# Hash-masked attention ahead of two expert layers: two of twelve score tiles transposed by TensorE in their own banks, a bias by a scalar operand, output scaling on GpSimd, and a new order of stages

## The chip, the cores and the metric

The program runs on one core of a Trainium2 chip. The metric is the device time of one execution in microseconds (us); three executions of the kernel before stand behind its median. A measurement of this kernel can tell about 0.3% (4.6 us) from no change.

## What is computed

Attention comes first, for 2 batches of 8 heads with 768 positions and 64 values per head. A position only attends to positions whose 6-bit hash bucket is the same:

```
q_bucket = bits of (q @ proj > 0);  k_bucket = bits of (k @ proj > 0)
mask     = q_bucket[:, None] == k_bucket[None, :]
scores   = where(mask, q @ k.T / 8, -1e9)
attn     = exp(scores - max(scores)); attn /= sum(attn) + 1e-9
out      = attn @ v
```

The result (1536 tokens of 512 values) goes through an expert layer that sums all eight experts, each token weighted by a matrix that is normalized eight times along rows and columns, and then through a second expert layer that gives each token that passes a threshold to one expert and adds its output. All results are float32.

## The kernel before, in words

`attention` handles 8 pairs of heads, one after the other. A pair has 12 **units**: (pair, head, block of 128 query rows), so 96 units in all. What happens to a unit, with the lines of the kernel before:

- `scores` (L243): four float32r matmuls of 384 columns write 128 x 768 scores into a two-bank PSUM tile, one of three (`p`, `s0`, `s1`). The hash mask is part of the product, so that a masked entry is off by 2^33 times the number of differing bits.
- `max_` (L252 to L254): VectorE reduces the row minimum, makes a scale (0 or -1) and a bias from it. Both small results are one value per partition.
- `exp_` (L261): ScalarE writes the float32 exponentials `P` to SBUF and gives the score tile back. `P` has three buffers.
- `hi` (L266) and `lo` (L269): ScalarE casts `P` to float16, GpSimd subtracts that from `P`; both halves go to `Pq` (six buffers).
- `trans` (L273): one DMA transpose on SP's queue turns both halves into `T` (nine buffers), 12 blocks of 128 x 128.
- `av` (L284, L285): twelve matmuls of `T` with the values, which are split into three bfloat16 parts with a column of ones; two units share a PSUM bank.
- `fin` (L295 to L298): for two units at once, VectorE sums the three parts, takes the reciprocal of the row sum and multiplies, into `X`. `xt` (L306, L307) transposes a finished pair's `X` for the expert layers.

Beside it runs the preparation of the next pair (`prep`): transposes of k and q into a score tile (`T`, L174), high parts on ScalarE (`A`, L180), low parts on VectorE (`Dd`, L184), copies to other partitions by DMA (`dup`, L188), the hash products into a score tile (`zz`, L199), their signs (`sgn`, L211), four small DMAs of them on SP (`sd`, L207), and the split of v (`v0` to `v3`, L203 and L230 to L232). The preparation takes score tiles from the same three.

The order on every engine is the order in which the program writes the stages down; each engine works through its own queue in that order and waits where a result is missing. A loop over `n` writes, for each step, the stages of `STEP[n % 2]`, each for the unit `n - lag`, and the pieces of preparation that the table `PLAN` hangs behind a place of the period of twelve steps. `scores` is written while a score tile is free, at most two units ahead (`AHEAD`). A step's list before, and how `give` and `take` hand the score tiles on:

```
STEP = [[('av', 7), ('max', 0), ('fin', 8), ('trans', 4), ('exp', 0), ('lo', 2), ('hi', 0), ('scores', -1)], ...]
while nxt <= min(n + AHEAD, N - 1) and free and ("sd", units[nxt][0]) in done:
    scores(units[nxt])
```

In the last two thirds of attention the loop also starts pieces of the expert layers' setup (`next(m)`); their weights are loaded on SP as well. After attention the expert layers fill the rest of the time.

Of the kernel before, what the change touches and what calls it, by code (L numbers as in the profile page):

```python
# [13 lines left out]
ALU = mybir.AluOpType  # L14
# [3 lines left out]
BIG = float(2.0 ** 33)  # L18
# [14 lines left out]

STEP = [[('av', 7), ('max', 0), ('fin', 8), ('trans', 4), ('exp', 0), ('lo', 2), ('hi', 0), ('scores', -1)], [('av', 7), ('max', 0), ('lo', 2), ('fin', 8), ('trans', 4), ('exp', 0), ('scores', -1), ('hi', 0)]]

PLAN = {12: 'Tk Ak1', 14: 'Ak0', 21: 'dk1', 25: 'Dk0 Dk1 Tq', 33: 'dk0', 37: 'Aq0 v0', 45: 'Dq0 Aq1', 49: 'Dq1', 59: 'z0', 60: 'z1', 66: 'dq1', 72: 'dq0 sg', 83: 'sd', 92: 'x v1', 94: 'v2', 95: 'v3'}
FIRST = "Tk Tq Ak0a Ak1a Dk0a Dk1a Ak0b Ak1b dk0 dk1 Dk0b Dk1b Aq0a Aq1a Dq0a Dq1a Aq0b Aq1b dq0 dq1 Dq0b Dq1b load1 za zb sga sgb sd load"
V0 = {1: "v0", 2: "v1", 3: "v2", 4: "v3"}  # L40

# [2 lines left out]
AHEAD = 2  # L44
M0 = range(39, 75, 3)
LD0, LDM, NTB, WARM = 3, 1, 9, 18


def attention(nc, tc, ident, q, k, v, proj, xT, m, go):
    with ExitStack() as c:  # L50
# [5 lines left out]
        free = ["p", "s0", "s1"]  # L56
        held = {}

        def take(key):
            t = held[key] = free.pop(0)  # L60
            return (pB if t == "p" else pS).tile([128, 2, 512], F32, tag=t, name=t, bufs=1)

        def give(key):
            free.append(held.pop(key))
# [84 lines left out]
        vs = {}  # L149

        def prep(i):

# [47 lines left out]

            def v0():
                nc.gpsimd.memset(vt[:, :, :, 0:1], 1.0)
                nc.vector.tensor_copy(out=vt[:, :, :, 1:65], in_=inp[i][2])  # L203
# [16 lines left out]
            for x, a in (("a", 0), ("b", 1)):  # L220
# [66 lines left out]
        def fin(u):  # L287
# [43 lines left out]
        stage = {"max": max_, "exp": exp_, "hi": hi, "lo": lo, "scores": scores, "trans": trans, "av": av, "fin": fin}  # L331
# [22 lines left out]
        for n in range(-1, N + AVLAG + 2):  # L354
            i, off = divmod(n + 13, 12)
            if off == 0 and i < NP:
                cur = prep(i)
            for j, (st, lag) in enumerate(STEP[n % 2]):
                u = n - lag
                if st == "scores":  # L360
                    while nxt <= min(n + AHEAD, N - 1) and free and ("sd", units[nxt][0]) in done:
                        scores(units[nxt])
                        nxt += 1
                elif 0 <= u < N and not (n > N and st in ("lo", "trans")) and not (st == "fin" and u >= N - AVLAG):
                    assert st != "av" or ("v3", units[u][0]) in done
                    stage[st](units[u])
                for op in PLAN.get(8 * off + j, "").split():
# [5 lines left out]
                if j == 7 and n in V0:  # L373
                    todo.extend((op, 0, p0[op]) for op in V0[n].split())
                prepare()
            if n >= 0 and n % 12 == LD0 and n // 12 + 2 < NP:
                ld.append(load(n // 12 + 2))
            if n % LDM == 0 and ld and next(ld[0], 0) == 0:
                ld.pop(0)
            if n in M0:  # L380
                next(m)
            if n == N:
                for u in units[N - 8:]:
                    if u in PP:
                        lo(u)
                for u in units[N - 8:]:
                    if u in PT and u not in TT:
                        trans(u)
                cp.close()
                cl.close()  # L390
                free[:] = ["p"]
            if 0 <= n - N < AVLAG:
                fin(units[n - AVLAG])
            if n == N + AVLAG:
                xt(NP - 1)
            if n >= N:
                next(m)
# [895 lines left out]
```

## Time and profile before

| | |
|---|---|
| runs | median 1525.09 us of 3 (1522.27 to 1526.89) |
| the profiled execution | 1523.56 us, its span 1521.7 us |
| mean granted TensorE clock | 0.975 of full speed |
| busy share of the span | TensorE 93%, VectorE 59%, GpSimd 59%, ScalarE 43% |
| attention | from the start to about 300 us |

The page gives the busy share of each engine over the whole span; the shares are a mean over attention and two expert layers, which have different limits, so the stretch of attention is read by itself. A stretch is here a period of twelve units, cut at the start of the row minimum that follows the hash signs (L211), which come once in twelve units. In windows by stretch, "DMA share" is packet time over 16 engines and can pass 1 where packets overlap.

### The profile page before, as it was taken

Reading aid. Unit: us, or ns where it says so; the run is one execution under the profiler, and the core shown is the slowest. Engines: PE = TensorE matmul, PEld = TensorE weight load, DVE = VectorE, ACT = ScalarE, POOL = GpSimd, SP = SyncE. Lnnn points to the kernel's source line nnn. Section 1 sums busy time; section 2 is a strip of 40 time slices with the busy share of each in tenths; the row PEclk is TensorE's granted clock in tenths of the full one; section 3 lists DMA queues with packets and bytes.
Section 4 is the critical chain, followed back from the end, with each engine's and each line's share of the span. In section 5 each row is a group of like instructions: output and inputs, shape, how many; then the busy total and the mean of one; then the engine's idle time right before and its main releaser. Section 6 shows DMA issues by size and latency. Waiting matters only on the chain.

```text
span 1521.7 us, 21039 instructions
## 1 busy us (share of the span) xinstructions
PE 1415.9 (93%) x7747; PEld 1240.7 (82%) x7747; DVE 899.5 (59%) x1778; ACT 653.8 (43%) x1015; POOL 895.9 (59%) x763
## 2 busy tenths in 40 slices
PE   6788777799999999999999999999999999998997
PEld 5677666578889889899898888989899898876886
DVE  7899989977625336254264736426244262555876
ACT  4777767742423333233333433333133232325665
POOL 3666666764665767657677656856667565512111
PEclk7999999999999999999999999999999999999999
DMA  5999999902121121211211412121211212527762
GB/s 148 192 207 202 203 200 183 171 30 82 57 83 56 56 83 57 83 56 56 84 56 56 164 58 56 56 83 56 83 56 56 84 56 84 194 67 241 258 249 69
DMA packets 224224, 166.27 MB, mean 109 GB/s; under 512 B 160023, under 2 KB 199063, under 8 KB 219761
## 3 DMA queue, kind: packets, MB, share of 16 engines
q1 hardware_dynamic: 219520, 154.69, 38.2%
q10 hardware_dynamic: 2448, 5.58, 1.7%
q0 software_dynamic: 2144, 4.57, 0.9%
q8 instruction: 63, 1.03, 0.3%
q14 instruction: 49, 0.39, 0.1%
HBM read 113.04 MB, written 7.77 MB: 79 GB/s over the span
## 4 chain that ended last, share of the span: by engine, by line
PE 59%; DVE 19%; POOL 15%; issue 3%; ACT 2%; DMA 1%; ACTq 0%; POOLq 0%; DVEq 0%
PE mp L1158 30%; PE mp L1041 15%; POOL w L473 8%; DVE m L252 5%; PE mp L935 4%; PE mp L954 4%; DVE m L254 3%; PE mp L1132 2%; DVE X L298 2%; POOL w L488 2%; POOL T L465 1%; DVE r L296 1%; POOL T L464 1%; DVE t L184 1%; PE mp L912 1%
## 5 line engine op out<-in xcount | busy, mean ns | idle before, releaser
L1158 PE MATMUL mp<-w,h 128*128 128x512 f32 x2160 | 501.5, 393 | 0.0
L1041 PE MATMUL mp<-x,w 128*128 128x384 f32 x2688 | 479.9, 337 | 14.5 <-POOL w L473 9.3
L1041 PEld LDWEIGHTS mp<-x,w 128*128 128x128 f32 x2688 | 467.2, 188 | 22.9 <-POOL w L473 14.1
L1158 PEld LDWEIGHTS mp<-w,h 128*128 128x128 f32 x2160 | 404.5, 188 | 85.8
L488 POOL TENSOR_TENSOR w<-raw,w 128x512 fp32r<-128x512 f32 x127 | 177.4, 1397 | 235.3 <-ACT w L487 235.3
L487 ACT CAST w<-raw 128x512 fp32r<-128x512 f32 x256 | 151.2, 620 | 193.3 <-PE mp L1158 175.1
L1175 DVE SCALAR_TENSOR_TENSOR acc<-mp,Pm,acc 128x512 f32<-128x512 f32 x78 | 54.1, 749 | 291.9 <-PE mp L1158 291.9
L269 POOL TENSOR_TENSOR Pq<-P,Pq 128x768 f16<-128x768 f32 x96 | 158.2, 1653 | 94.7 <-ACT Pq L266 87.0
L473 POOL TENSOR_TENSOR w<-raw,w 128x512 fp32r<-128x512 f32 x124 | 128.9, 1060 | 95.5 <-ACT w L469 95.5
L1085 ACT ACTIVATE h<-ca 128x768 fp32r<-128x768 f32 x64 | 54.3, 848 | 235.4 <-DVE ca L1049 235.4
L473 POOL TENSOR_TENSOR w<-T,w 128x1024 fp32r<-128x1024 f32 x62 | 149.7, 2415 | 0.0
L471 ACT CAST w<-T 128x1024 fp32r<-128x1024 f32 x64 | 67.3, 1052 | 174.2 <-POOL T L466 170.4
L243 PE MATMUL s<-k,t 128*128 128x384 f32 x264 | 70.4, 393 | 37.0 <-ACT P L261 31.7
L284 PE MATMUL b<-vt,T 128*128 128x193 bf16 x576 | 98.8, 261 | 2.5 <-DMA T<-Pq 2.5
L1049 DVE TENSOR_TENSOR u<-mp,p 128x384 f32<-128x384 f32 x64 | 35.6, 556 | 103.2 <-ACT p L1056 61.0
L285 PE MATMUL b<-vt,T 128*128 128x129 bf16 x576 | 95.1, 229 | 0.0
L488 DVE TENSOR_TENSOR w<-raw,w 128x512 fp32r<-128x512 f32 x129 | 84.3, 696 | 12.7 <-ACT w L487 12.5
L261 ACT ACTIVATE P<-s,m 128x768 f32<-128x768 f32 x66 | 65.4, 991 | 55.0 <-DVE m L254 35.1
L243 PEld LDWEIGHTS s<-k,t 128*128 128x128 f32 x264 | 48.7, 211 | 46.4 <-ACT P L261 38.8
L266 ACT CAST Pq<-P 128x768 f16<-128x768 f32 x96 | 79.9, 832 | 6.2 <-DMA T<-Pq 3.8
L1089 DVE SCALAR_TENSOR_TENSOR h<-ca,h 128x768 fp32r<-128x768 f32 x64 | 66.5, 1039 | 19.3 <-ACT h L1085 19.3
L1049 DVE TENSOR_TENSOR u<-mp,u 128x384 f32<-128x384 f32 x128 | 66.7, 553 | 18.6 <-PE mp L1041 14.1
(268 smaller groups left out, 1924.5 us busy)
## 6 DMA issues: line engine op xcount, KB each, us to landing
raw<-in_moe_w_dram SPq DMA_DIRECT2D x128, 256.0 KB
raw<-in_moe_w_dram SPq DMA_DIRECT2D x64, 512.0 KB
raw<-in_moe_w_dram SPq DMA_DIRECT2D x32, 1024.0 KB
k<-in_k_dram SPq DMA_DIRECT2D x16, 192.0 KB
q<-in_q_dram SPq DMA_DIRECT2D x16, 192.0 KB
v<-in_v_dram SPq DMA_DIRECT2D x8, 384.0 KB
out_dram<-acc SPq DMA_DIRECT2D x2, 1536.0 KB
k<-k ACTq DMA_DIRECT2D x14, 192.0 KB
```

The lines of the kernel that those rows point to most:

```text
L243: nc.tensor.matmul(ps[:, hf, 0:384], lhsT=a[s][h][:, js], rhs=b[s][h][:, 384 * hf:384 * hf + 384], start=n == 0, stop=n == 1)
L252: nc.vector.tensor_reduce(out=m[:, 0, c], in_=w2(ps), axis=AX.XY, op=ALU.min)
L266: nc.scalar.copy(out=PT[u][:, 0], in_=PP[u])
L269: nc.gpsimd.tensor_tensor(out=PT[u][:, 1], in0=PP.pop(u), in1=PT[u][:, 0], op=ALU.subtract)
L284: nc.tensor.matmul(o, lhsT=t[:, n, :], rhs=vt[:, h, ORDER[n], :], start=n == 0, stop=False)
L285: nc.tensor.matmul(o[:, 0:129], lhsT=t[:, 6 + n, :], rhs=vt[:, h, ORDER[n], 0:129], start=False, stop=n == 5)
L473: tl(out=w[:, 1, c0:c1], in0=src, in1=wf[:, 0, c0:c1], op=ALU.subtract)
L487: nc.scalar.copy(out=w[:, 0, :], in_=v)
L488: eng.tensor_tensor(out=w[:, 1, :], in0=v, in1=w[:, 0, :].bitcast(F32), op=ALU.subtract)
L1041: nc.tensor.matmul(dst, lhsT=w[:, i_, 2 * blk + c, :], rhs=x[:, x_, c, :], start=n == 0, stop=n == 5)
L1049: nc.vector.tensor_tensor(out=o, in0=a, in1=b_, op=ALU.add)
L1158: nc.tensor.matmul(ys[t], lhsT=h[:, a, 128 * t:128 * t + 128], rhs=w[:, i_, :], start=i == 0 and n == 0, stop=i == 7 and n == 2)
```

## The change

- In each pair, the units 2 and 8 (`QP`; all but the last two units of the program may be among them) keep their score tile after `exp_`. TensorE transposes the float32 `P` back into that tile (`qtrans`, six transposes), ScalarE casts it from there to `T` (`qhi`), VectorE writes the low half to `T` (`qlo`), and only then the tile is given back. These units have no `hi`, no `lo` and no DMA transpose.
- The bias is made by a `tensor_scalar` with the row minimum as both input and scalar operand, in place of a `scalar_tensor_tensor`.
- The multiplication at the end of `fin` goes to GpSimd, except for the last seven units.
- The lists of stages and `PLAN` are new; `PLAN` now hangs on the stages' names. `lo` comes one step after its unit and not two, `trans` five steps and not four.

```diff
-STEP = [[('av', 7), ('max', 0), ('fin', 8), ('trans', 4), ('exp', 0), ('lo', 2), ('hi', 0), ('scores', -1)], ...
+STEP = [[('max', 0), ('exp', 0), ('trans', 5), ('ql', 2), ('fin', 8), ('hi', 0), ('qh', 1), ('av', 7), ('qt', 0), ('lo', 1), ('scores', -1)],
+        [('trans', 5), ('ql', 2), ('max', 0), ('exp', 0), ('scores', -1), ('fin', 8), ('qh', 1), ('hi', 0), ('lo', 1), ('av', 7), ('qt', 0)]]
-PLAN = {12: 'Tk Ak1', 14: 'Ak0', ...
+PLAN = {(0, 'max'): 'Tk', (0, 'lo'): 'Ak1', (1, 'ql'): 'Ak0', ...
+QP = (2, 8)
-            nc.vector.scalar_tensor_tensor(out=m[:, 2, c], in0=m[:, 0, c], scalar=BIG / 2, in1=m[:, 0, c], op0=ALU.is_lt, op1=ALU.mult)
+            nc.vector.tensor_scalar(out=m[:, 2, c], in0=m[:, 0, c], scalar1=BIG / 2, scalar2=m[:, 0, c], op0=ALU.is_lt, op1=ALU.mult)
             nc.scalar.activation(out=v2(P), in_=w2(F.pop(u)), func=AF.Exp, bias=m[:, 2, c], scale=m[:, 1, c])
-            give(u)
+            if u not in QU:
+                give(u)
+        def qtrans(u):
+            F[u] = pair(held[u])
+            P = PP.pop(u)
+            for n in range(6):
+                nc.tensor.transpose(F[u][:, n // 3, 128 * (n % 3):128 * (n % 3) + 128], P[:, 128 * n:128 * n + 128], ident)
+        def qhi(u):
+            PT[u] = tp.tile([128, 12, 128], F16, tag="T", name="T", bufs=NTB)
+            nc.scalar.copy(out=parts(PT[u], 0), in_=w2(F[u]))
+            TT.add(u)
+        def qlo(u):
+            nc.vector.tensor_tensor(out=parts(PT[u], 1), in0=w2(F.pop(u)), in1=parts(PT[u], 0), op=ALU.subtract)
+            give(u)
-            nc.vector.tensor_tensor(out=X[i][:, j - 1:j + 1, 64 * h:64 * h + 64], in0=r,
+            (nc.vector if late else nc.gpsimd).tensor_tensor(out=X[i][:, j - 1:j + 1, 64 * h:64 * h + 64], in0=r,
+        QU.update(u for n, u in enumerate(units[:N - 2]) if n % 12 in QP)
```

Where the order moves, three places. VectorE before, from the hash signs of one period on, two units and one `fin`:

```order
193 L211 TENSOR_SCALAR sg<-s_1294,scl 128x768
194 L252 TENSOR_REDUCE m<-s_1316 128x1
195 L253 TENSOR_SCALAR m<-m 128x1
196 L254 SCALAR_TENSOR_TENSOR m<-m 128x1
197 L252 TENSOR_REDUCE m<-p 128x1
...
200 L295 TENSOR_SCALAR m<-b 128x2
201 L296 TENSOR_REDUCE r<-b 128x128
202 L297 RECIPROCAL m<-m 128x2
203 L298 TENSOR_TENSOR X<-r,m 128x2x64
```

VectorE in the change, from the same place on (L218 is the signs, L259 to L261 the row minimum, scale and bias, L322 to L324 `fin`, L288 `qlo`):

```order
189 L218 TENSOR_SCALAR sg<-s_1338,scl 128x768
190 L259 TENSOR_REDUCE m<-p 128x1
191 L260 TENSOR_SCALAR m<-m 128x1
192 L261 TENSOR_SCALAR m<-m 128x1
193 L322 TENSOR_SCALAR m<-b 128x2
194 L323 TENSOR_REDUCE r<-b 128x128
195 L324 RECIPROCAL m<-m 128x2
...
199 L288 TENSOR_TENSOR T<-s_1402,T 128x768
200 L238 CAST vt<-r_1041 128x12x64
```

The multiplication into `X` is gone from this queue, the bias is another instruction, and `qlo` stands ahead of the cast of v.

TensorE in the change, at unit 2 of a pair (L277 is `qtrans`, L250 `scores`, L181 the transposes of q):

```order
254 L311 LDWEIGHTS T
255 L311 MATMUL b<-vt,T 128x193
256 L312 LDWEIGHTS T
257 L312 MATMUL b<-vt,T 128x129
258 L277 MATMUL s_711<-ident,P 128x128 x6
259 L250 MATMUL p<-k_137,t_129 128x384 x2
260 L250 MATMUL p<-k_141,t_133 128x384 x2
261 L181 MATMUL s_744<-ident,q 128x128 x6
262 L311 LDWEIGHTS T
```

Two `av` stand ahead of the transposes and only one `scores` behind them: of the three score tiles one is kept by the unit itself and one by the preparation of q.

GpSimd in the change, with what each waits for (L296 is `lo`, L325 the multiplication into `X`, L237 and L239 the split of v):

```order
63 L296 TENSOR_TENSOR Pq<-P,Pq 128x768 [waits DMAHW5_49,Activation_49,Pool_49]
64 L325 TENSOR_TENSOR X<-r,m 128x2x64 [waits DVE_49,PE_49]
65 L237 TENSOR_TENSOR r_1041<-v,vt 128x768
66 L239 TENSOR_TENSOR vt<-r_1041,vt 128x12x64 [waits DVE_49]
67 L296 TENSOR_TENSOR Pq<-P,Pq 128x768 [waits DMAHW0_49,Activation_49]
68 L325 TENSOR_TENSOR X<-r,m 128x2x64 [waits DVE_49]
```

Here a multiplication that waits for VectorE now stands between the `lo` of successive units, and the two GpSimd steps of the split of v stand next to each other, with VectorE's cast between them in time.

## Rows read from the trace of the kernel before

**Rows 1.** The chain that ended last, 0 to 330 us: shares by line.
```profile
by line: DVE m L252 23.6%; DVE m L254 15.1%; DVE X L298 8.8%; DVE r L296 6.1%; issue 4.8%; DVE t L184 4.7%; DVE k L184 4.4%; DVE m L253 4.1%; PE mp L1041 2.8%; DVE sg L211 2.3%; DMA T<-Pq 1.8%; DVE w L473 1.8%; PE s L199 1.8%; PE mp L632 1.
```
**Rows 2.** Windows: length, busy PE, PEld, DVE, ACT, POOL, clock, DMA share, GB/s.
```profile
45.52:78.14 32.62, 25.48 (x229) 21.93 (x226) 31.71 (x73) 24.49 (x32) 20.76 (x15) 1.00 1.06 196
...
147.81:182.48 34.67, 25.95 (x230) 22.24 (x227) 33.76 (x73) 25.74 (x34) 22.97 (x16) 1.00 1.10 201
182.48:222.52 40.04, 30.91 (x244) 25.83 (x242) 35.67 (x80) 26.37 (x34) 25.60 (x24) 0.91 1.08 208
...
256.75:293.77 37.02, 29.71 (x278) 24.84 (x276) 36.27 (x75) 26.17 (x30) 28.56 (x18) 1.00 1.00 176
```
**Rows 3.** Lines of VectorE: count, shortest/median/longest ns, first and last start.
```profile
L253 DVE TENSOR_SCALAR m<-m x96: 152/153/160, 23.0 to 294.7; 128x1 f32<-128x1 f32 x96
L254 DVE SCALAR_TENSOR_TENSOR m<-m x96: 147/594/1614, 23.1 to 294.7; 128x1 f32<-128x1 f32 x96
L770 DVE TENSOR_SCALAR rt<-rt x12: 232/319/1458, 846.2 to 1369.2; 128x8 f32<-128x8 f32 x12
```
**Rows 4.** Timeline of VectorE and GpSimd: start us, us.
```profile
148.69 1.66 POOL L269 TENSOR_TENSOR Pq<-P,Pq 128x768 f16<-128x768 f32 x1
148.78 1.58 DVE L254 SCALAR_TENSOR_TENSOR m<-m 128x1 f32<-128x1 f32 x1
...
219.80 3.40 POOL L269 TENSOR_TENSOR Pq<-P,Pq 128x768 f16<-128x768 f32 x2 [2.07 <-ACT Pq L266]
...
221.51 1.00 DVE L211 TENSOR_SCALAR sg<-s,scl 128x768 fp32r<-128x768 f32 x1
```
**Rows 5.** Groups by form, 50 to 560 us: count, busy us, mean ns, idle before.
```profile
L269 POOL TENSOR_TENSOR Pq<-P,Pq 128x768 f16<-128x768 f32 x88 | 145.0, 1654 | 72.5 <-ACT Pq L266 65.1 <-POOL r L230 2.8 <-issue 1.4
L266 ACT CAST Pq<-P 128x768 f16<-128x768 f32 x87 | 72.4, 832 | 6.0 <-DMA T<-Pq 3.8
L261 ACT ACTIVATE P<-s,m 128x768 f32<-128x768 f32 x58 | 57.5, 991 | 38.6 <-DVE m L254 22.3 <-DVE m L295 7.6 <-DVE desc L582 2.6
L254 DVE SCALAR_TENSOR_TENSOR m<-m 128x1 f32<-128x1 f32 x86 | 55.1, 640 | 0.0
L298 DVE TENSOR_TENSOR X<-r,m 128x128 f32<-128x128 f32 x47 | 35.9, 764 | 1.6
L252 DVE TENSOR_REDUCE m<-s 128x1 f32<-128x768 f32 x58 | 54.9, 947 | 0.7 <-PE s L243 0.5
L184 DVE SCALAR_TENSOR_TENSOR t<-s,t 64x384 fp32r<-64x384 f32 x16 | 8.9, 554 | 0.4
L180 ACT ACTIVATE t<-s 64x384 fp32r<-64x384 f32 x16 | 7.7, 482 | 0.2
L466 POOL TENSOR_TENSOR T<-raw,T 128x256 f32<-128x256 f32 x15 | 11.1, 737 | 0.0
```
**Rows 6.** Timeline of TensorE: `scores`, first of `av`, `scores`, transposes of k.
```profile
156.54 0.97 PE L243 MATMUL p<-k,t 128*128 128x384 f32 x4 [2.39 <-ACT P L261]
...
157.35 0.26 PE L284 MATMUL b<-vt,T 128*128 128x193 bf16 x1
...
158.18 0.94 PE L243 MATMUL s<-k,t 128*128 128x384 f32 x4
...
159.82 0.82 PE L174 MATMUL s<-ident,k 128*128 128x128 f32 x6
```
**Rows 7.** Windows of the hash products (L199) alone, TensorE busy us.
```profile
147.81:182.48 34.67, 3.04 (x16) 2.75 (x16) 1.00 1.10 201
```
**Rows 8.** Timeline of VectorE and ScalarE: an unblocked row minimum and its exponential.
```profile
84.51 0.94 DVE L252 TENSOR_REDUCE m<-s 128x1 f32<-128x768 f32 x1
...
85.82 0.99 ACT L261 ACTIVATE P<-s,m 128x768 f32<-128x768 f32 x1 [1.41 <-DVE m L254]
```
**Rows 9.** Timeline of SP's queue, 116 to 130 us; then a landing, from the chain.
```profile
116.43 13.24 SPq L273 DMA_TRANSPOSE T<-Pq  x7
...
18.53 2.75 DMA k<-sg
```

More of the change, by code (lines that the diff above doesn't have):

```diff
@@ L32 @@
 WB = 8
-STEP = [[('av', 7), ('max', 0), ('fin', 8), ('trans', 4), ('exp', 0), ('lo', 2), ('hi', 0), ('scores', -1)], [('av', 7), ('max', 0), ('lo', 2), ('fin', 8), ('trans', 4), ('exp', 0), ('scores', -1), ('hi', 0)]]
-PLAN = {12: 'Tk Ak1', 14: 'Ak0', 21: 'dk1', 25: 'Dk0 Dk1 Tq', 33: 'dk0', 37: 'Aq0 v0', 45: 'Dq0 Aq1', 49: 'Dq1', 59: 'z0', 60: 'z1', 66: 'dq1', 72: 'dq0 sg', 83: 'sd', 92: 'x v1', 94: 'v2', 95: 'v3'}
+STEP = [[('max', 0), ('exp', 0), ('trans', 5), ('ql', 2), ('fin', 8), ('hi', 0), ('qh', 1), ('av', 7), ('qt', 0), ('lo', 1), ('scores', -1)], [('trans', 5), ('ql', 2), ('max', 0), ('exp', 0), ('scores', -1), ('fin', 8), ('qh', 1), ('hi', 0), ('lo', 1), ('av', 7), ('qt', 0)]]
+PLAN = {(0, 'max'): 'Tk', (0, 'lo'): 'Ak1', (1, 'ql'): 'Ak0', (2, 'lo'): 'Dk0', (2, 'qt'): 'dk1', (4, 'scores'): 'Dk1', (4, 'fin'): 'v0', (4, 'lo'): 'Tq', (4, 'qt'): 'Aq0', (5, 'fin'): 'dk0', (5, 'hi'): 'Dq0', (5, 'qt'): 'Aq1', (6, 'qt'): 'dq1', (7, 'ql'): 'Dq1', (7, 'qt'): 'dq0', (8, 'exp'): 'z0', (8, 'qh'): 'z1', (9, 'exp'): 'sg', (10, 'qh'): 'sd', (11, 'qh'): 'x', (11, 'qt'): 'v1 v2 v3'}
 FIRST = "Tk Tq Ak0a Ak1a Dk0a Dk1a Ak0b Ak1b dk0 dk1 Dk0b Dk1b Aq0a Aq1a Dq0a Dq1a Aq0b Aq1b dq0 dq1 Dq0b Dq1b load1 za zb sga sgb sd load"
@@ L46 @@
 LD0, LDM, NTB, WARM = 3, 1, 9, 18
+QP = (2, 8)
+VE = 'DD'
 def attention(nc, tc, ident, q, k, v, proj, xT, m, go):
@@ L57, in attention, with pair @@
         held = {}
+        def pair(t):
+            return (pB if t == "p" else pS).tile([128, 2, 512], F32, tag=t, name=t, bufs=1)
         def take(key):
             t = held[key] = free.pop(0)
-            return (pB if t == "p" else pS).tile([128, 2, 512], F32, tag=t, name=t, bufs=1)
+            return pair(t)
         def give(key):
@@ L149, in attention @@
         vs = {}
+        VC = {"A": nc.scalar.copy, "D": nc.vector.tensor_copy, "P": nc.gpsimd.tensor_copy}
         def prep(i):
@@ L202, in v0 @@
                 nc.gpsimd.memset(vt[:, :, :, 0:1], 1.0)
-                nc.vector.tensor_copy(out=vt[:, :, :, 1:65], in_=inp[i][2])
+                VC[VE[0] if i else "D"](out=vt[:, :, :, 1:65], in_=inp[i][2])
             def sd():
@@ L230, in prep @@
                 "v1": lambda: nc.gpsimd.tensor_tensor(out=r1, in0=inp[i][2], in1=vt[:, :, :, 1:65], op=sub),
-                "v2": lambda: nc.vector.tensor_copy(out=vt[:, :, :, 65:129], in_=r1),
+                "v2": lambda: VC[VE[1] if i else "D"](out=vt[:, :, :, 65:129], in_=r1),
                 "v3": lambda: nc.gpsimd.tensor_tensor(out=vt[:, :, :, 129:193], in0=r1, in1=vt[:, :, :, 65:129], op=sub)})
             return r
-        X, PT, M, F, PP, O, TT = {}, {}, {}, {}, {}, {}, set()
+        X, PT, M, F, PP, O, TT, QU = {}, {}, {}, {}, {}, {}, set(), set()
         def scores(u):
@@ L261, in exp_, with parts @@
             nc.scalar.activation(out=v2(P), in_=w2(F.pop(u)), func=AF.Exp, bias=m[:, 2, c], scale=m[:, 1, c])
+            if u not in QU:
[5 more added lines that the diff above has]
+                nc.tensor.transpose(F[u][:, n // 3, 128 * (n % 3):128 * (n % 3) + 128], P[:, 128 * n:128 * n + 128], ident)
+        def parts(t, a):
+            return v2(t[:, 6 * a:6 * a + 6].rearrange("p a b -> p (a b)"))
+        def qhi(u):
[4 more added lines that the diff above has]
+            nc.vector.tensor_tensor(out=parts(PT[u], 1), in0=w2(F.pop(u)), in1=parts(PT[u], 0), op=ALU.subtract)
             give(u)
@@ L285, in av, with fin @@
                 nc.tensor.matmul(o[:, 0:129], lhsT=t[:, 6 + n, :], rhs=vt[:, h, ORDER[n], 0:129], start=False, stop=n == 5)
-        def fin(u):
+        def fin(u, late=False):
             i, h, j = u
@@ L297, in fin @@
             nc.vector.reciprocal(out=m[:, 0, :], in_=m[:, 4, :])
-            nc.vector.tensor_tensor(out=X[i][:, j - 1:j + 1, 64 * h:64 * h + 64], in0=r,
-                                    in1=m[:, 0, :].unsqueeze(2).to_broadcast([128, 2, 64]), op=ALU.mult)
+            (nc.vector if late else nc.gpsimd).tensor_tensor(out=X[i][:, j - 1:j + 1, 64 * h:64 * h + 64], in0=r,
+                                                             in1=m[:, 0, :].unsqueeze(2).to_broadcast([128, 2, 64]), op=ALU.mult)
         def xt(i):
@@ L330, in attention @@
         N = len(units)
-        stage = {"max": max_, "exp": exp_, "hi": hi, "lo": lo, "scores": scores, "trans": trans, "av": av, "fin": fin}
+        QU.update(u for n, u in enumerate(units[:N - 2]) if n % 12 in QP)
+        stage = {"qt": qtrans, "qh": qhi, "ql": qlo, "max": max_, "exp": exp_, "hi": hi, "lo": lo, "scores": scores, "trans": trans, "av": av, "fin": fin}
         cur, todo, done, nxt = {}, [], {("sd", 0)}, 0
@@ L365, in attention @@
                     assert st != "av" or ("v3", units[u][0]) in done
-                    stage[st](units[u])
-                for op in PLAN.get(8 * off + j, "").split():
+                    if st[0] == "q" and units[u] in QU or st[0] != "q" and not (st in ("hi", "lo", "trans") and units[u] in QU):
+                        stage[st](units[u])
+                for op in PLAN.get((off, st), "").split():
                     if op == "x":
@@ L372, in attention @@
                         todo.append((op, i, cur[op]))
-                if j == 7 and n in V0:
+                if j == len(STEP[0]) - 1 and n in V0:
                     todo.extend((op, 0, p0[op]) for op in V0[n].split())
@@ L392, in attention @@
             if 0 <= n - N < AVLAG:
-                fin(units[n - AVLAG])
+                fin(units[n - AVLAG], True)
             if n == N + AVLAG:
```

## The prediction

> **What bounds the kernel now.** I read the chain of waits over attention first. Of its time, 24% is the row minimum (L252), 15% the one-element bias (L254), 9% the multiplication into `X` (L298): VectorE all the way down, with small pieces of other engines [rows 1]. The windows by period say the same: in 34.67 us VectorE is busy for 33.76, TensorE for 25.95, ScalarE for 25.74, GpSimd for 22.97 [rows 2]. So attention runs at VectorE's pace, about 2.9 us a unit; whatever VectorE loses is time won until another limit is met.
>
> Then I asked why an instruction on one element costs so much. The scale (L253) and the bias (L254) both work on 128 x 1. The first takes 152 to 160 ns in all 96 cases; the second 147 to 1614, 640 on the mean [rows 3, 5]. The timeline shows the cause: it starts 0.09 us after a subtraction on GpSimd and ends with it [rows 4]. `scalar_tensor_tensor` reads two tensors from SBUF and waits for GpSimd's running instruction. `X` does the same, at 764 ns [rows 5].
>
> **The change, part by part**, for one period of twelve units.
>
> *Bias by a scalar operand.* Does the new form wait too? Two rows bear on it. The signs (L211) read a scalar operand from SBUF and their data from PSUM; at 221.51 they ran their 1.00 us in the middle of GpSimd's two subtractions, without delay [rows 4]. And L253, the same operation on one element of SBUF without a scalar operand, never waits [rows 3]. No row has both. Bounds: 0.15 us (L253) and 0.64 (as before). The nearest row is L770, with a scalar operand: 0.23 at its shortest [rows 3]. I take 0.23: 12 x (0.64 - 0.23) = 4.9 us off VectorE.
>
> The Trainium skill, page "SBUF — State Buffer", section "Who interferes with whom", speaks against it: `tensor_scalar` on VectorE can enter modes that use the port pair it shares with GpSimd, and then the second to start blocks. L770, on eight elements, agrees with up to 1458 ns; L253 does not show it on one [rows 3]. By the rule the sum would be that of the third rival below.
>
> *`X` on GpSimd.* 6 x 0.76 = 4.6 us off VectorE. On GpSimd, 128 x 256 takes 0.74, 128 x 768 1.65 [rows 5]; a straight line through both gives 0.51 at 128 x 128, with ends at 0.15 (as L253, nothing smaller is seen) and 0.74. It adds 6 x 0.5 = 3.1 us there. Its wait for VectorE holds up the `lo` behind it, but `lo` now comes one step earlier, and in the walk below each `lo` ends before the third exponential after it wants its buffer of `P`.
>
> *Two units by TensorE.* Each adds six transposes, 0.82 us by those of k [rows 6]; a cast on ScalarE in place of one as long (0.83 from SBUF; the exponential, which reads PSUM, takes 0.99 [rows 5]; I take 0.83); and a 768-element pass on VectorE, 0.95 as the row minimum [rows 5]. It takes 1.65 off GpSimd and a transpose off SP: seven in a row took 13.24 us, 1.9 each [rows 9].
>
> *Sums.* VectorE 33.8 - 4.9 - 4.6 + 1.9 = 26.2. TensorE 25.95 + 1.6 = 27.6 (the period at a full clock). ScalarE 25.7. GpSimd 23.0 - 3.3 + 3.1 = 22.8. The transposes 10 x 1.9 = 19 of SP's time where 12 took 23. No engine is above 27.6, so if work were always at hand a period would fall to 28. It won't be: each engine has its queue in a fixed order, and a unit of the two keeps its score tile longer.
>
> *The new order, walked through.* I set down one period by the order of the queues. Steps: a score tile is ready 0.97 after its matmuls start, TensorE is free for the next after 0.82; `av` 0.83 [rows 6]; the hash products 1.5 per half [rows 7]; from the start of a row minimum to its exponential 1.31 [rows 8]; exponential 1.0, cast 0.75 from start to start, one pair of `A` 0.9 [rows 5]. Zero is the end of the exponential of a pair's first unit (0).
> - ScalarE: `A` of k 0.9, cast 0.75, exponential of 1: 2.65.
> - Only now is unit 3's tile free: scores, row minimum, exponential, 3.4: 6.1. Unit 2 keeps its tile and k the third, so unit 4 waits for this one: scores to 7.1; q's transposes 0.7, its `A` 1.0 and, behind it, exponential 4: 9.85. Unit 5 takes the same tile: 3.4, to 13.3.
> - From here TensorE has its fill: scores, two `av`, scores, half the hash products, scores, the other half: 7.1, to 20.4. The signs wait for the last: 21.4.
> - Row minimum and exponential of 9: 23.7. ScalarE: cast of 8, cast of 9, exponential of 10: 26.2. `xt` and its copy 1.8, exponential of 11: 29.0; cast, `A` of the next k, exponential of 12: 31.7.
>
> VectorE's cast of v (0.55, two buffers in SBUF) comes right behind a `fin`, just as GpSimd starts the new multiplication: up to 0.5 more. I take **32.2 us** where 34.7 stands now. The walk's ends are the largest sum (28) and 34.2: SP sends the four small DMAs of the signs one after another from 21.4, and the next pair's first scores stand at 27.8; a landing took 2.75 us after its signs [rows 9], and two more behind running transposes would push everything behind them.
>
> *The stretches.* Five periods, 78.14 to 256.75, took 178.6 us, one of them 40.04 [rows 2], because casts waited there for transposes to free `Pq`. With ten transposes for twelve I keep 2 us of that excess: 5 x 32.2 + 2 = 163, **-15.6**. The period before (32.62) has no `xt`; walk without it 31.1, **-1.5**; the start, with few blocked instructions, **-1.5**. The last stretch (fifteen units in 37.0 us, 2.47 each) has little preparation: VectorE falls to some 1.65 a unit, then ScalarE (1.75) and TensorE (1.8) lead; at 2.1 with the order's waits 31.5, **-5.5**. What follows is unchanged and starts earlier; the last seven multiplications stay on VectorE. Sum **-24**. The profiled execution took 1523.56, 1.5 below the median; I forecast **1500**.
>
> **The rivals.**
> - *The queues run ahead, and the sums decide.* For: the walk has TensorE idle for 4 us and VectorE for 6 in each period, and pieces may slide. Against: the score tiles are held in order, and from 2.65 to 13.3 each step waits for the one before. 29.2 a period: 5 x 29.2 = 146, -32.6; -3, -2, and -8 at the end: 1478.
> - *The tile that is kept and the signs' DMAs cost more.* At 34 a period, with the 2 us of excess: -6.6, and -1, -1, -4.4 for the rest: 1510.5.
> - *The scalar operand waits for GpSimd's port* (other side). L770 was delayed by up to 1.2 us over its shortest; against it stand L211 at 221.51 and L253. The place is the bias (L261 of the change), the price 0.41 us more in twelve places, 4.9 a period, now in a chain that goes through scores, minimum, bias and exponential without slack: 32.2 + 4.9 = 37.1 if all of it counts. It decides from 34.7 - 32.2 = 2.5 us on, six of the twelve. At nine: 35.9 a period: 5 x 35.9 + 2 = 181.5, +2.9; +1 and +1 before; the end at 2.5 a unit, +0.5: 1529; with all twelve +6 more, 1535.
>
> **How the numbers follow.** The forecast has 0.66, with its own range 1490 to 1508 (period 30.5 to 33.5). Queues that run ahead 0.13, the tile and DMAs 0.11, the scalar operand 0.08, nothing seen at all 0.02. A measurement of this kernel can tell about 0.3% (4.6 us) from no change, so faster is below 1520.5, slower above 1529.7. Faster: the first three but for a twentieth, 0.86. Same: that twentieth and the mild end of the third rival, 0.06. Slower: 0.08. The range for 8 in 10 leaves out the third rival and half of the first: 1481 to 1517.
>
> **What would show it.** The bias line: a median near 0.23 us, no value above 0.5; one near 0.6 is the third rival. `X` on GpSimd about 0.5 us. VectorE's busy time 26 us a period, with idle time ahead of the signs and the row minima, and TensorE's, ScalarE's and VectorE's shares between 80 and 88%. Idle time of TensorE ahead of unit 4's and unit 5's scores, put down to the exponential. DMA share below 1. The expert layers as long as before: a difference there of over 3 us would make the sum wrong, even if the total were right. A period below 30.5 says the order has more slack than the walk, one above 34 that a tile or a DMA has become the limit.

## The result, and the profile after

The change takes **1504.39 us** (median of 5 runs, 1502.49 to 1512.36) where the kernel before, run beside it, takes 1523.81 (5 runs, 1519.94 to 1526.89): a ratio of **0.9883** [0.9861, 0.9904], so 1.0 to 1.4% faster. The forecast was 1500, with a range of 1481 to 1517. The profiled execution took 1504.39 us with a span of 1502.6, 19.1 less than before. From the last row minimum to the end of the span it is 1228.6 us (before: 1228.0), so all of the gain lies in attention, as forecast.

The chain of waits over 0 to 330 us, by line. In the change L259 is the row minimum, L261 the bias, L268 the exponential, L250 the scores, L206 the hash products, L296 GpSimd's `lo`, L311 the `av`:

```profile
by line: ACT P L268 12.4%; PE p L250 7.7%; PE mp L1070 7.5%; DMA T<-Pq 7.5%; issue 6.3%; DVE m L259 5.9%; PE s L206 5.7%; POOL Pq L296 4.6%; PE b L311 4.3%; ACT Pq L293 3.9%; PE s L250 2.9%; PE b L312 2.8%; DVE sg L218 2.0%; ACT k L187 2.0%
```

Before, VectorE held the chain with 24, 15 and 9% at three of its lines [rows 1]. Now no engine does: the row minimum has 5.9%, the bias is not among the lines shown, and the DMA transposes (`T<-Pq`) have risen from 1.8% to 7.5%.

The windows by period (columns as in [rows 2]: length, busy time of PE, PEld, DVE, ACT, POOL, clock, DMA share, GB/s):

```profile
49.04:81.36 32.32, 27.39 (x236) 24.63 (x234) 26.32 (x69) 24.77 (x32) 21.91 (x19) 0.95 1.02 189
81.36:112.67 31.31, 26.59 (x241) 23.91 (x239) 26.41 (x68) 25.57 (x33) 21.87 (x19) 1.00 1.01 188
112.67:144.64 31.97, 26.88 (x241) 23.87 (x239) 26.42 (x68) 25.56 (x33) 21.90 (x19) 1.00 1.02 189
144.64:177.25 32.61, 26.79 (x241) 23.77 (x239) 26.41 (x69) 25.65 (x33) 21.88 (x19) 1.00 1.08 214
177.25:211.80 34.55, 28.63 (x241) 25.11 (x239) 27.05 (x75) 25.56 (x33) 22.73 (x26) 0.95 1.11 209
211.80:245.69 33.89, 27.99 (x242) 25.31 (x239) 27.53 (x77) 25.57 (x33) 23.24 (x34) 0.95 1.01 160
245.69:273.98 28.29, 25.91 (x247) 23.11 (x244) 23.95 (x69) 24.70 (x29) 22.97 (x20) 1.00 1.02 169
```

VectorE fell from 33.8 us a period to 26.4 [rows 2]; TensorE, ScalarE and VectorE are now busy for 79 to 85% of the three periods from 81.36 to 177.25. The last stretch shrank most: 28.29 us for 37.02.

The lines whose prices were forecast (columns as in [rows 3]): the bias, the multiplication into `X`, the low half and the cast of the two units, GpSimd's `lo`:

```profile
L261 DVE TENSOR_SCALAR m<-m x96: 201/204/206, 23.4 to 275.0; 128x1 f32<-128x1 f32 x96
L325 POOL TENSOR_TENSOR X<-r,m x44: 388/400/634, 51.0 to 276.9; 128x128 f32<-128x128 f32 x44
L288 DVE TENSOR_TENSOR T<-s,T x15: 946/948/948, 35.0 to 273.1; 128x768 f16<-128x768 f32 x15
L284 ACT CAST T<-s x15: 787/790/799, 32.5 to 271.2; 128x768 f16<-128x768 f32 x15
L296 POOL TENSOR_TENSOR Pq<-P,Pq x80: 1632/1650/1762, 26.4 to 278.8; 128x768 f16<-128x768 f32 x80
```

The bias takes 201 to 206 ns in all 96 cases; before it took 147 to 1614 [rows 3].

The waits of 40 to 290 us (who waits, for whom; total us, times, longest):

```profile
POOL X L325 <- DVE m L324: 61.9, 28, 4.0
PEld p L250 <- ACT P L268: 36.8, 32, 2.1
ACT P L268 <- DVE m L322: 29.1, 15, 4.0
PE p L250 <- ACT P L268: 27.0, 29, 1.7
DVE sg L218 <- PE s L206: 16.7, 7, 3.0
```

The scores wait for an exponential, that is for a score tile, as the walk had it, and the signs wait for the hash products. One link of the fourth period (from 144.64 us, 32.61 long), from the chain in order of time (start, us, what):

```profile
143.71 1.02 DVE sg L218
144.73 0.88 DVE m L259
...
147.04 1.56 POOL r L237
148.61 0.80 issue
149.44 1.61 POOL vt L239
...
153.02 3.10 POOL Pq L296 x2
156.19 0.33 POOL X L325
156.54 7.70 DMA T<-Pq
164.28 0.26 PE b L311
```

Behind the signs the chain runs through GpSimd's two steps of the split of v, then two `lo`, and then a transpose that lands 7.7 us later. That is not the price of one transpose (1.9, [rows 9]): by SP's timeline three transposes and two loads of 256 KB were issued just ahead of it, from 148.08 us on.

### The profile page after: what moved, and what is told of

Same layout as the page of the kernel before. It is cut to its first block, busy times and chain, and to the rows that moved or that the text cites. A ratio compares the mean times of both kernels' runs of the same rounds, so it can differ in the third digit from the quotient of the medians.

```text
span 1502.6 us, 21166 instructions
## 1 busy us (share of the span) xinstructions
PE 1413.7 (94%) x7843; PEld 1245.4 (83%) x7843; DVE 846.1 (56%) x1750; ACT 652.3 (43%) x1015; POOL 885.4 (59%) x791
## 4 chain that ended last, share of the span: by engine, by line
PE 64%; POOL 16%; ACT 6%; DVE 6%; issue 4%; DMA 3%; ACTq 0%; POOLq 0%; DVEq 0%; SPq 0%
PE mp L1187 31%; PE mp L1070 15%; POOL w L502 8%; PE mp L983 4%; PE mp L964 4%; ACT P L268 3%; PE mp L1161 2%; PE p L250 2%; DMA T<-Pq 2%; POOL w L517 2%; POOL T L494 1%; POOL T L493 1%; DVE m L259 1%; PE s L206 1%; POOL Pq L296 1%
## 5 line engine op out<-in xcount | busy, mean ns | idle before, releaser
L296 POOL TENSOR_TENSOR Pq<-P,Pq 128x768 f16<-128x768 f32 x80 | 131.0, 1651 | 30.8 <-ACT Pq L293 28.7
L311 PE MATMUL b<-vt,T 128*128 128x193 bf16 x576 | 92.6, 256 | 3.1 <-DMA T<-Pq 3.1
L312 PE MATMUL b<-vt,T 128*128 128x129 bf16 x576 | 90.3, 226 | 0.0
L250 PE MATMUL p<-k,t 128*128 128x384 f32 x208 | 53.3, 381 | 30.3 <-ACT P L268 30.0
L1078 DVE TENSOR_TENSOR cb<-mp,u 128x384 f32<-128x384 f32 x128 | 70.4, 550 | 8.2 <-PE mp L1070 7.2
L250 PEld LDWEIGHTS p<-k,t 128*128 128x128 f32 x208 | 36.7, 201 | 40.8 <-ACT P L268 40.7
L1118 DVE SCALAR_TENSOR_TENSOR h<-cb,h 128x768 fp32r<-128x768 f32 x64 | 69.1, 1080 | 0.8
```

The costliest lines, as they stand in the source:

```text
L250: nc.tensor.matmul(ps[:, hf, 0:384], lhsT=a[s][h][:, js], rhs=b[s][h][:, 384 * hf:384 * hf + 384], start=n == 0, stop=n == 1)
L296: nc.gpsimd.tensor_tensor(out=PT[u][:, 1], in0=PP.pop(u), in1=PT[u][:, 0], op=ALU.subtract)
L1078: nc.vector.tensor_tensor(out=o, in0=a, in1=b_, op=ALU.add)
L1118: nc.vector.scalar_tensor_tensor(out=h_[:, 1, :], in0=c_.rearrange("p a t -> p (a t)"), scalar=0.0, in1=h_[:, 0, :].bitcast(F32), op0=ALU. ...
```

## The experiments

Twelve kernels, in three groups; each group had its own runs of the kernel before, with medians of 1522.52, 1524.42 and 1522.14 us. Periods are distances between the starts of the hash signs.

**1. What each part is worth inside the change.** My theory was that all three parts take their share off VectorE's path and that the two units matter least of them.

The bias undone:

```diff
-            nc.vector.tensor_scalar(out=m[:, 2, c], in0=m[:, 0, c], scalar1=BIG / 2, scalar2=m[:, 0, c], op0=ALU.is_lt, op1=ALU.mult)
+            nc.vector.scalar_tensor_tensor(out=m[:, 2, c], in0=m[:, 0, c], scalar=BIG / 2, in1=m[:, 0, c], op0=ALU.is_lt, op1=ALU.mult)
```

> The changed kernel with one part undone: the bias is made by scalar_tensor_tensor again, everything else as in the change. Theory (VectorE's waits for GpSimd were the limit and the bias is the largest of them): the instruction goes back from 0.20 us to about 0.6, a period grows by 2 to 5 us from the 32.9 seen now, since some of it falls into VectorE's idle time ahead of the signs; 1515 to 1530 us. Rival (the new order and the two units off the DMA path give the gain): the bias is hidden in VectorE's idle time, 1508 or less.

Measured: 1516.47 us, ratio 0.9963 [0.9952, 0.9975]; periods 33.5, 33.4, 34.8, 33.5, 36.4, 35.9. So the bias is worth 12 us here. Its old form again waits:

```profile
L261 DVE SCALAR_TENSOR_TENSOR m<-m x96: 148/428/1507, 22.2 to 286.5; 128x1 f32<-128x1 f32 x96
```

The multiplication into `X` back on VectorE:

```diff
-            (nc.vector if late else nc.gpsimd).tensor_tensor(
+            nc.vector.tensor_tensor(
```

> The changed kernel with the multiplication into X on VectorE for all units. Theory: it waits for GpSimd's subtraction again (mean 0.7 us, six in a period), about half of it on the chain: a period longer by 1.5 to 3 us, 1510 to 1522 us. Rival (X on GpSimd costs as much as it gives, since lo stands behind its wait): within 4 us of the change, 1500 to 1508.

Measured: 1509.21 us, 0.9917 [0.9893, 0.994]. Worth about 5 us; the interval just meets that of the change, and the time lies between the two ranges expected.

No unit by TensorE, the new order kept:

```diff
-QP = (2, 8)
+QP = ()
```

> The changed kernel with no unit transposed by TensorE (all twelve go over Pq and the DMA transpose), order of stages kept. Theory (these two units give little: VectorE was the limit and their tile is held longer): 1498 to 1510 us, and the start of attention about 3 us shorter. Rival (they give the gain by relieving the transposes, SP and GpSimd): 1515 or more, with casts or av waiting for transposes.

Measured: **1528.68 us**, 1.0042 [1.0028, 1.0057], slower than the kernel before; periods 35.0, 34.8, 34.2, 39.0, 35.4, 37.8. My theory's expectation was missed by far. In the new order, with the bias and `X` in place, taking away the part that I had thought least of costs 24 us, more than the whole gain of 19. The chain of 0 to 330 us names what took over, GpSimd's `lo` and the transposes:

```profile
by line: DMA T<-Pq 14.1%; POOL Pq L296 12.0%; issue 11.0%; ACT P L268 7.9%; DVE m L259 5.3%; ACT Pq L293 4.4%; PE s L206 3.8%; PE s L250 3.2%; PE mp L1070 2.8%; PE b L311 2.6%; POOL r L237 2.4%; DMA q<-in_q_dram 1.9%; DVE w L502 1.8%; PE p 
```

These 24 us are not the price of the transposes alone. The first period is already long, with a low DMA rate (columns as above), and in the chain of that period (48 to 83 us) GpSimd's `lo` has 28.8% and no transpose appears:

```profile
48.06:83.05 34.99, 27.81 (x223) 25.02 (x221) 24.59 (x66) 25.40 (x32) 24.94 (x21) 0.90 0.99 179
```

Run 2 has the same twelve units on the DMA transposes and the same bias, but the old order and `X` on VectorE, and takes 13 us less than this one (1515.76). So with twelve transposes the new order or `X` on GpSimd does harm; which of them was not tried.

**2. The bias alone, on the kernel before.** If VectorE is the only limit, it should give its whole 5 us a period.

```diff
-            nc.vector.scalar_tensor_tensor(out=m[:, 2, c], in0=m[:, 0, c], scalar=BIG / 2, in1=m[:, 0, c], op0=ALU.is_lt, op1=ALU.mult)
+            nc.vector.tensor_scalar(out=m[:, 2, c], in0=m[:, 0, c], scalar1=BIG / 2, scalar2=m[:, 0, c], op0=ALU.is_lt, op1=ALU.mult)
```

> The kernel before with the bias edit alone. Theory: VectorE loses 12 x 0.44 = 5.3 us of a period of 34.7 and the rest follows until the next wait: period 30.5 to 33, 1495 to 1512 us. Rival (the old order can't use it, something else in it is as long): 1515 to 1524, no change.

Measured: 1515.76 us, 0.9955 [0.9938, 0.9973]; periods **30.6, 31.1**, 35.3, 35.4, 40.5, 33.9. The total falls on the rival's side, the first two periods on the theory's: they show what the bias can give. From 105.8 us on the gain is gone, and VectorE is busy for only 30.6 of 35.3 us:

```profile
44.08:74.70 30.62, 24.45 (x222) 21.52 (x221) 28.84 (x71) 23.67 (x31) 21.25 (x15) 1.00 1.04 199
74.70:105.80 31.10, 25.82 (x228) 22.13 (x227) 29.32 (x72) 25.66 (x34) 22.97 (x16) 1.00 1.10 198
105.80:141.13 35.33, 25.98 (x228) 22.18 (x227) 30.58 (x71) 25.57 (x34) 22.85 (x15) 1.00 1.09 207
176.51:217.02 40.51, 32.00 (x242) 26.97 (x240) 31.31 (x78) 26.72 (x34) 25.69 (x23) 0.87 1.08 203
```

The waits of that kernel, 105 to 255 us, name the transposes twice, ahead of the casts that need a free `Pq` and ahead of `av`:

```profile
ACT Pq L266 <- DMA T<-Pq: 15.3, 5, 5.1
...
PEld L284 <- DMA T<-Pq: 9.0, 10, 2.2
```

From about 130 us on, within the first of the long periods, the loads of the experts' weights (256 KB each) run on SP's queue beside the transposes. Two explanations: they delay the transposes in SP's queue, or all DMA engines are full.

**3. The loads of the weights on another queue.** In the kernel with the bias alone, and in the change, the eight loads are issued by ScalarE:

```diff
-        return [lambda c=c: nc.sync.dma_start(out=v[:, c], in_=src[:, c]) for c in range(v.shape[1])]
+        q = nc.scalar if n < 2 else nc.sync
+        return [lambda c=c: q.dma_start(out=v[:, c], in_=src[:, c]) for c in range(v.shape[1])]
```

> The kernel before with the bias edit, and the first eight loads of expert weights (256 KB each) issued from ScalarE's queue in place of SP's, in the same places of the program. In the run with the bias edit alone the periods without such loads took 30.6 and 31.1 us, those with them 35.3, 35.4 and 40.5. Theory A (SP's queue, which issues the transposes in order, is what the loads cost): the three late periods fall to 31 to 34, total 1500 to 1508. Theory B (the DMA engines themselves are full, wherever a load is issued): no change, 1512 to 1518.

Measured: 1517.03 us, 0.9949 [0.9932, 0.9966]; periods 30.6, 31.7, 37.0, 42.9, 35.5, 35.2. No gain, although it gave SP's queue room: its rows in the timeline, waits among them, cover all of the 70 us from 110 to 180 with the bias alone and some 64 of them here.

> The changed kernel with the same eight loads issued from ScalarE's queue. Theory A (SP's queue): its periods four to six of 32.6, 34.6 and 33.9 us fall by about 1 us each, 1499 to 1502. Theory B (the DMA engines are full): 1503 to 1507. Against both: each issue takes about half a microsecond of ScalarE, which is not the limit.

Measured: 1502.81 us, 0.9886 [0.9848, 0.9925]: the change's own ratio, between the two ranges expected. Its periods four to six, 32.6, 33.7 and 32.5, are 0, 0.9 and 1.3 us shorter than the change's, which is nearer to theory A, but the total does not show it. So the loads' place in SP's queue is not what lengthens the late periods with the bias alone; in the change it may be worth a microsecond or two, less than the interval can tell. The Trainium skill, page "DMA: Bandwidth & Descriptors", section "Rules for kernel authors", says that spreading DMAs over issuing engines does not add bandwidth, since all run on the same 16 DMA engines; the totals of these two runs agree (1517.03 against 1515.76, 1502.81 against 1504.39).

**4. Transposes or GpSimd?** The two units take both a transpose and a `lo` away. Two kernels with the bias alone take away one each, for the units 2 and 8 of a pair. Both give these units' halves two buffers of their own, and both have seven buffers `T` for nine. These seven serve ten units of a period in the first and twelve in the second, but in neither do the waits of SP's transposes (40 to 290 us) name `av`, which is what frees a buffer. Both leave work out, so what they compute is not the whole attention. Without the transposes:

```diff
         def trans(u):
+            if u in QU:
+                PT[u] = PT[u].rearrange("p a (n c) -> p (a n) c", n=6)
+                TT.add(u)
+                return
```

> The kernel before with the bias edit alone, and the units 2 and 8 of each pair are not transposed at all (their float16 halves go to av as they are, from two buffers of their own; T has seven buffers instead of nine to make room). Left out: ten sixteenths of nothing else, only these transposes. The bias edit alone took 1515.8 us, with periods of 35.3, 35.4 and 40.5 us from the fourth on, where the chain stands on the transposes. Theory A (the second limit is the transposes, by the DMA engines): without two of twelve those periods fall to 31 to 33 and the time to 1500 to 1506. Theory B (the second limit is GpSimd, whose subtractions are late): periods stay within 1 us of 35.3 and the time at 1512 to 1517.

Without the low halves on GpSimd:

```diff
         def lo(u):
+            if u in QU:
+                PP.pop(u)
+                return
```

> The counterpart: the kernel before with the bias edit alone, and GpSimd leaves out the low half of the units 2 and 8 of each pair (it stays zero in two buffers of their own; T has seven buffers here too); all transposes run. GpSimd has 3.3 us less in each period. Theory A (transposes): periods from the fourth on stay at 34 to 36 and the time at 1511 to 1517. Theory B (GpSimd): they fall to 31 to 33 and the time to 1500 to 1506. If this and the run without the transposes both fall, the buffers of the float16 halves (eight for twelve units instead of six) are what both share.

Measured: without the transposes **1495.99 us**, 0.9825 [0.9808, 0.9841], periods 30.6, 31.1, 31.0, 33.4, 34.2, 35.2; without the low halves 1512.75, 0.9937 [0.9915, 0.9959], periods 30.4, 35.0, 32.4, 35.1, 37.6, 36.1. Theory A holds: with the bias alone, the second limit is the transposes. The first run gains 20 us on the bias alone, more than expected (1500 to 1506), though its last three periods did not reach 31 to 33. Taking 3.3 us of each period off GpSimd gives 3 us, and the intervals overlap. The windows, first of the kernel without the low halves, where GpSimd is busy for 19.8 of 35.1 us:

```profile
141.73:176.83 35.10, 26.63 (x228) 23.44 (x227) 28.41 (x73) 25.80 (x33) 19.80 (x14) 0.95 1.07 210
```

then of the kernel without two transposes, with GpSimd at 22.9 as before:

```profile
105.91:136.95 31.04, 25.16 (x228) 22.16 (x227) 29.25 (x71) 25.74 (x34) 22.95 (x16) 1.00 1.07 199
```

The DMA share is over 1 and the rate near 200 GB/s in both. With the bias alone they are so in the short periods of 30.6 and 31.1 us too, which have the same twelve transposes and no loads of weights (run 2). I read it so: the engines move what they can in all of them, and a period is as long as the work in it. That is an inference; no run changed what the engines can move. How much one transpose is of that work: the DMA view of three periods with the bias alone (105.80 to 217.02 us, 36 units), with the packets first and then each queue's share of 16 engines:

```profile
DMA packets 63554, 23.04 MB, mean 207 GB/s; under 512 B 58264, under 2 KB 62631, under 8 KB 63543
...
q1 hardware_dynamic: 62583, 20.54, 97.7%
q10 hardware_dynamic: 960, 2.36, 9.7%
...
T<-Pq SPq DMA_TRANSPOSE x37
```

and the same three periods without two transposes in each (105.91 to 204.54):

```profile
DMA packets 51402, 19.97 MB, mean 203 GB/s; under 512 B 46127, under 2 KB 50479, under 8 KB 51391
...
q1 hardware_dynamic: 50431, 17.47, 95.3%
q10 hardware_dynamic: 960, 2.36, 12.5%
...
T<-Pq SPq DMA_TRANSPOSE x30
```

Both queues together, 1.074 x 111.2 = 119.4 us against 1.078 x 98.6 = 106.3: a difference of 13.1 us. The program has six transposes fewer in three periods; as the windows cut, the views count 37 issued against 30, and one load of q more (7 against 6). So one transpose is 13.1 / 7 to 13.1 / 6, **1.9 to 2.2 us** of all 16 engines, an estimate from the shares. Twelve of them are 22 to 26 us of a period, and 14 to 17 us of other transfers stand beside them.

**5. The two units alone, on the kernel before**, in its old order:

> The kernel before with the two units by TensorE alone (old lists and places; bias and multiplication as before). Theory A (two limits one behind the other, VectorE's waits first): VectorE gains 1.9 us a period and stays the limit, so no gain where the transposes were hidden, and the few microseconds of the period of 40 us: 1518 to 1528. Theory B (the transposes are the limit by themselves): 1500 to 1510.

Measured: 1528.54 us, 1.0049 [1.003, 1.0069], slower, half a microsecond beyond theory A's range; periods 35.3, 34.6, 34.7, 36.5, 37.1, 34.5. VectorE's line is back at the head of the chain of 80 to 260 us, and the DMA engines have room:

```profile
by line: DVE m L259 27.3%; DVE m L261 16.4%; DVE r L323 6.8%; DVE t L191 6.2%; DVE X L325 6.1%; DVE k L191 5.0%; DVE T L288 4.9%; DVE m L260 4.1%; issue 3.8%; DVE sg L218 3.4%; PE s L250 2.9%; PE p L181 2.7%; PE s L277 2.2%; PE b L311 1.8%;
```

A window of it (columns as above):

```profile
115.15:149.82 34.67, 26.94 (x240) 23.66 (x238) 33.01 (x75) 25.54 (x35) 19.64 (x13) 1.00 0.92 190
```

So the two limits lie right behind each other: the bias alone gains 0.5%, the two units alone lose 0.5%, and all three parts together gain 1.2 to 1.4%.

**6. The order.** All parts, with the old lists and places (the stages of the two units added):

```diff
-STEP = [[('max', 0), ('exp', 0), ('trans', 5), ('ql', 2), ...
+STEP = [[('av', 7), ('max', 0), ('ql', 2), ('fin', 8), ('trans', 4), ('exp', 0), ('lo', 2), ('qh', 1), ('hi', 0), ('scores', -1), ('qt', 0)], ...
```

> All parts of the change (bias, X on GpSimd, two units by TensorE) with the old lists of stages and the old places of the preparation; the three new stages are put at comparable places (qtrans last in its step, qhi one step later, qlo two). Theory now (the limit behind VectorE is the path of the transposes, and the parts free both): the parts do most of it, 1500 to 1512 us. Rival (the parts only work in the new order): 1515 or more.

Measured: 1502.47 us, 0.9861 [0.9835, 0.9887]; periods 31.9, 32.8, 31.8, 33.3, 33.6, 32.2. The new order is worth nothing that can be measured. But the second pair's signs start at 44.6 us with the old order (before: 44.5) and at 48.1 with the new one. To see whether the unit by TensorE in the first pair costs these 3.5 us, or the order:

```diff
-        QU.update(u for n, u in enumerate(units[:N - 2]) if n % 12 in QP)
+        QU.update(u for n, u in enumerate(units[:N - 2]) if n % 12 in QP and n >= 12)
```

> The changed kernel with no unit of the first pair transposed by TensorE. The start, to the second pair's hash signs, took 48.1 us against 44.5 before. Theory (units 2 and 8 keep a score tile while TensorE still runs at half its clock there): the signs come at 45 to 46.5, total 1500 to 1503. Rival (the new order of the preparation costs it, not the two units): signs at 47.5 or later, total 1503 to 1507.

Measured: 1504.0 us, 0.9877 [0.9857, 0.9898], signs at 48.2; without any unit by TensorE, in the new order too (run 1), they start at 48.1. It is the order, lists and places together.

**7. A third unit by TensorE**, in the old order:

```diff
-QP = (2, 8)
+QP = (2, 6, 10)
```

> All parts with the old lists and places, and three units of a pair (2, 6, 10) by TensorE instead of two. With two it took 1502.5. Theory A (the transposes still hold the late periods, which were 33.3 and 33.6 us): nine transposes for ten take 1 us off such a period: 1496 to 1500. Rival (a score tile that is kept by its unit holds up the scores behind it, and that is now the limit): a third kept tile adds 1 to 2 us a period: 1506 to 1515.

Measured: 1520.06 us, 0.9984 [0.9975, 0.9994]; periods 34.4, 34.3, 34.4, 34.4, 36.9, 37.6. The rival was right, and more so than expected: a period is 34.4 us, with nine transposes, at a DMA share of 0.92 and of 1.02 alike.

```profile
113.69:148.07 34.38, 27.30 (x246) 24.39 (x245) 28.43 (x68) 25.69 (x33) 20.49 (x19) 1.00 0.92 181
148.07:182.47 34.40, 27.39 (x246) 24.45 (x245) 28.44 (x68) 25.70 (x33) 20.47 (x19) 1.00 1.02 196
```

No engine is above 83% there. That the kept score tile does it fits, and was not tried by itself. The chain of 80 to 260 us names a part of it that is something else, VectorE's second cast of v:

```profile
120.35 1.62 POOL r L237
121.99 1.98 DVE vt L238
```

It takes 1981 ns at its median here and 550 in the change, and stands so in the chain of four periods: it starts while GpSimd's `lo` runs, which comes right behind GpSimd's step of the split. That is 1.4 us of a period. No version that computes the whole attention ran measurably faster than the change.

## Why the prediction was right, and where it was not

**The prices were right.** Bias 0.23 taken, 0.204 measured; `X` on GpSimd 0.5 and 0.40; the cast 0.83 and 0.79; the low half 0.95 and 0.948. VectorE's sum was to be 26.2 and is 26.4, TensorE's 27.6 and 26.9, ScalarE's 25.7 and 25.6, GpSimd's 22.8 and 21.9. The third rival, the scalar operand that waits for GpSimd, fell: not one of 96 took over 0.206. Run 1 shows that it would have mattered, by the 12 us of the old form. The rule of the Trainium skill (page "SBUF — State Buffer", section "Who interferes with whom") that `cast` and `tensor_scalar` can enter the modes that contend with GpSimd does not show for `tensor_scalar` on one element; on the cast of v it does, in the start:

```profile
26.37 1.64 POOL L296 TENSOR_TENSOR Pq<-P,Pq 128x768 f16<-128x768 f32 x1 [20.57 <-ACT Pq L293]
26.75 1.76 DVE L210 CAST vt<-v 128x768 bf16<-128x768 f32 x1
```

The cast, 0.54 us at its median, begins inside the `lo` and ends at 28.51, about its own length after the `lo` ends at 28.01.

**The stretches.** Five periods were to give -15.6 and gave 164.3 for 178.6, **-14.3**. The three of full clock stand at 31.3, 32.0 and 32.6, where I had 32.2; the two late ones at 34.6 and 33.9 have 4.4 us of excess over 32, for the 2 that I kept. The tail was to give -5.5 and gave **-8.8** (signs to last row minimum, 38.0 and 29.2): TensorE is busy there for 25.9 of 28.3 us, so its sum of 1.8 a unit nearly decides, and the 0.3 that I had added for the order's waits hardly came. The start was to give -1.5 and gave **+3.6**, the period after it -0.3 for -1.5. Together -19.8 for -24; behind attention the span is 0.6 longer than before.

**The step that was mis-sized** is the start: "with few blocked instructions, -1.5". I priced the blocked instructions and not the places in which the new order writes the preparation. Run 6 shows that the new order, lists and places together, costs the 3.5 us. What in it does is only seen, not tried. In the first 21.5 us TensorE is busy for 12.0 to 12.1 us at a granted clock of 0.84 before, with the old order and in the change. From 21.5 to 30 us the clock is 0.75 before, 0.73 with the old order and 0.50 in the change, which is the lower of its two levels (1.2 GHz) throughout:

```profile
21.50:30.00 8.50, 5.38 (x14) 3.85 (x14) 6.76 (x13) 4.94 (x8) 3.49 (x4) 0.50 0.58 175
```

Two of its scores take 1.65 us there, with idle time ahead of each (1.43 and 1.20 in the same stretch with the old order, 0.94 to 0.97 at the full clock); in the old order k's transposes stand between them.

**The step that failed in its reason, though not in its sum**, is the account of the two units: "It takes 1.65 off GpSimd and a transpose off SP", and with it "the transposes 10 x 1.9 = 19 of SP's time where 12 took 23". I counted the transposes as one queue's time, well below a period, and so took the units for a small cost to VectorE. Even as one queue's time that was too low: beside 23 us of transposes, SP's rows have some 10 us of loads and signs in each period (about 20 of the 70 us from 110 to 180 before). And the DMA share in [rows 2] already stood at 1.00 to 1.10 in the stretches shown, and I forecast that it would fall below 1. It is 1.01 to 1.11. A transpose costs about 2 us of all 16 engines and shares them with 14 to 17 us of loads and copies in the late periods. With the bias alone twelve of them fit into 31 us; with the loads of the weights beside them three periods take 35.3, 35.4 and 40.5 though VectorE is busy for 30.6 to 31.3 (run 2), and without two of them these take 31.0, 33.4 and 34.2 (run 4). So the forecast came out because the change relieves both limits, the one that I saw and the one that I did not. That the second gave way by about as much as the walk needed is luck: but for the excess of the 40 us period, nothing in the prediction's sum stands for it. I take the 40 us period, which I had put down to transposes that hold `Pq`, for the visible end of this limit; that was not tried by itself.

**The walk.** It gave 32.2 and the periods are near it, and TensorE's waits ahead of the scores are put down to the exponential, as it says. It is not confirmed by that: the old order, which I did not walk, gives 31.8 to 33.6 as well, and the DMA share stands at 1.01 to 1.08. Which of the score tiles and the DMA engines ends a period of 32 us stays open. With three units (run 7) it is not the DMA engines, since the period is the same at 0.92 and at 1.02. With none, in the new order (run 1), the first period hangs on GpSimd's `lo`, and the transposes enter the chain of attention later.

## What to carry to other kernels

When the chain of waits points at one engine throughout, look also for the resource that is full without standing in the chain: here the DMA share was 1.00 to 1.10 in every period while the transposes had 1.8% of the chain. A share over 1 alone does not say that it sets the pace, since short periods have it too; a run that leaves the work out does. Of two limits that lie so close, a part tried by itself can look worth little or harmful; try the parts together and then take each away from the whole. And price a new order by its worst place too, the start among them, not only by the steady period.

## What the hardware showed that was not expected

- A one-element `tensor_scalar` with its scalar operand in SBUF takes 204 ns, 50 more than the one without (L260: 154), and never waited for GpSimd in 96 cases.
- A cast of v (128 x 768, float32 to bfloat16) took 546 to 556 ns in all sixteen cases before (L203, L231). In the change the first of them took up to 1762 (1768 in the run without the first pair's unit), and with the bias alone, in the old order, the second took 832 at its median and up to 2011: whether a cast meets an instruction of GpSimd changes with every shift in time.
- Moving eight loads of 256 KB from SP's queue to ScalarE's changed neither total by more than the noise (1517.03 against 1515.76, 1502.81 against 1504.39), with the DMA share over 1.
- Taking 3.3 us of 23 off GpSimd in each period changed nothing measurable, though the chain of 0 to 330 us named its `lo` with 5.7% in the kernel with the bias alone:

```profile
by line: DMA T<-Pq 13.3%; issue 8.2%; ACT P L261 5.7%; POOL Pq L269 5.7%; DVE m L252 5.6%; PE s L243 5.1%; PE mp L1041 4.5%; ACT Pq L266 4.1%; DVE t L184 3.7%; PE s L199 3.6%; PE b L284 3.3%; ACT k L180 2.7%; PE p L199 2.5%; DVE X L298 2.5%
```
